# A fused retention and gated-MLP kernel: the first layer of batch 1 in seven half-size products, and the output product of batch 0 moved behind its gate

## The chip, the cores and the metric

The kernel runs on one core of a Trainium2 chip. The metric is the device time of one execution in microseconds. The kernel before took 510.05 us (median of three runs, 509.23 to 510.31). Five engines of the core work side by side, each on its own stream of instructions: TensorE (PE, with its weight loads shown apart as PEld), VectorE (DVE), ScalarE (ACT), GpSimd (POOL) and SyncE (SP, which here issues the DMAs).

## The reference, cut to what matters

```python
# q, k, v: (8 batches, 8 heads, 576 tokens, 64)
scores = q @ k.T / sqrt(64)
ret = scores * D                     # D[h, i, j] = gamma_h ** (i - j) for i >= j, else 0
x = (ret @ v) -> (8, 576, 512)       # heads side by side
h = relu(x @ w_in)                   # w_in (512, 1024)
u, v = h[..., :512], h[..., 512:]
v_n = (v - mean(v)) / sqrt(var(v) + 1e-6)
v_s = w_spatial @ v_n + b_spatial    # w_spatial (576, 576), over the tokens
out = (u * v_s) @ w_out              # w_out (512, 512)
```

All in float32. No softmax stands between the scores and their product with v, so the first half can be computed chunk by chunk with a carried state.

## The kernel before, in words

**One batch.** The 576 tokens are four chunks of 128 and a tail of 64. A chunk is loaded by DMA (tiles qk, kn, vv), its q and k are scaled, its scores are taken and masked (at), and the state of the heads (sh, st, decayed in dec) carries what earlier chunks leave. These are 64-row matmuls, in groups of 16 or 32, in the banks r. The result x goes to SBUF transposed. Then come the first layer (u and v), v normalised (vn, and vt1 for the tail), the spatial product with w_spatial (wsp, wtl) and the gate (u * v_s, called g below), and the output product, whose blocks are stored from the tiles o, vl, tail and u.

**Accuracy.** PE multiplies rounded numbers (type F32R). Each operand is kept as a rounded half and the rest, and each product is three matmuls: high by high, high by low, low by high (`mm3`, L571). So before a product takes an operand, ACT copies it into the rounded half and another engine subtracts that (type fp32r in the rows): a *split*.

**Two ways to a dense product.** The *plain* way takes a 512 x 512 product block by block: a tile of u is 12 matmuls of 288 columns, a tile of v for one chunk 12 of 512. The other takes it as *seven products of half size* instead of eight (`product_chain`, L860, parts A to E; `product`, L836): sums and differences of quarters of the weights, made once (`made_weight`, L336), by sums and differences of quarters of x or g, made in every batch (`plain_quarter`, L327, `summed_quarter`, L330). A product for one half of the rows is 6 matmuls, of 256 columns for v and 288 for u and the output; its results are added up by DVE in the tile u. Rows of such products read the tiles quarter, part, places and slot.

**Which batch goes which way.** `PLAIN = 2`: batches 0 and 1 have a plain first layer. Batch 0's output product is plain too (`f_chain`, L812); the output of batch 1 and all of batches 2 to 7 are seven products.

**The order.** It is written out by hand. `ORDER` (L44) holds batches 0 and 1 and the start of 2, `STEADY` is repeated for each later one, `LAST` ends it. Each word names a chain, and each time it stands there, `run` (L942) takes one step of that chain: one group of instructions. Every engine runs its instructions in that order, so the order of words sets every engine's queue; nothing is reordered later. The words used here (the table of makers is at L907): d, D, T, S load a chunk, a weight, a tail, w_spatial; w and s split weights; q, k, t, g, p, b are the steps of the retention; v is a chunk of v with its normalising; U, V, G, P are batch 0's u, spatial product, gate and split; y and X are u and the spatial product of a plain batch 1; F is a plain output product; W is a part of seven products (batch, kind, half, part); R and K make plain and summed quarters of x, Y and Z those of g; A makes weights of the seven products. Letters at the end (p, v, a) choose the engine: POOL, DVE, ACT. `BANKS` gives each product its PSUM bank m0 to m3.

**Rooms.** SBUF is full, so tiles share tags. The two big rooms slot0 and slot1 hold x and g of a batch in turns; `room` (L337) for making the weights of the output lies in slot0, the raw weights pass through `raw` and slot1.

All instructions are issued through one wrapper, so the trace gives line 204 for each (209 in the changed kernel); rows are told apart by tiles. In rows, m stands for the four banks, r for those of the retention, win and wout for the weights, slot for x or g of a batch, kn and qk for loaded chunks, qsct and tail for the tail.

Of the kernel before, what the change touches and what calls it, by code (L numbers as in the profile page):

```python
# [29 lines left out]
PLAIN = 2  # L30
WHOLE = 1
# [12 lines left out]
    d.0.0 z.40.1 c.a z.22.1 d.0.0 z.17.1 d.0.0 z.10.1 D.1.1 d.0.1 z.16.1 d.0.1 z.24.1 d.0.1 z.13.1 z.15.1 D.1.0  # L44
    z.39.1 g.0.0 D.1.2 g.0.0 q.0.0.p D.1.3 k.0.0.v d.0.2 p.0.0.va z.19.1 p.0.0.va z.26.1 D.0.1 z.23.1 w.1.1.vp
    p.0.0.va b.0.0 w.1.1.vp z.20.1 b.0.0 w.1.1.vp D.0.0 b.0.0 b.0.0 p.0.0.va d.0.3 w.1.1.vp k.0.1.p g.0.1 b.0.0
    D.0.2 w.1.1.vp z.2.1 p.0.0.va z.5.1 q.0.1.p b.0.0 p.0.1.aa w.1.1.vp z.33.1 p.0.1.aa w.1.0.vp z.27.1 g.0.1 z.25.1
    z.1.1 z.42.1 w.1.0.vp z.21.1 z.11.1 w.1.0.vp z.41.1 w.1.2.pp z.30.1 z.32.1 w.1.0.vp p.0.1.aa z.3.1 w.1.2.pp
    z.34.1 z.35.1 w.1.0.vp z.18.1 w.1.3.vp b.0.1 S z.4.1 b.0.1 w.1.3.vp w.1.0.vp T.0 z.8.1 p.0.1.aa b.0.1 S w.1.3.vp
    w.1.0.vp b.0.1 w.1.2.pp z.31.1 b.0.1 z.9.1 w.1.3.vp z.29.1 c.t z.37.1 k.0.2.a q.0.2.p z.38.1 w.1.2.pp g.0.2  # L50
    b.0.1 d.1.0 z.6.1 w.1.1.vp w.1.2.pp z.7.1 p.0.1.aa d.1.0 p.0.2.aa z.0.1 w.0.0.vp p.0.2.aa z.12.1 v.0.0 w.1.3.vp
    w.1.2.pp w.0.0.vp p.0.2.aa z.14.1 w.1.2.pp g.0.2 b.0.2 w.0.0.vp z.36.1 w.1.3.vp S v.0.1 w.0.1.vp p.0.2.aa
    w.1.3.vp w.0.0.vp v.0.0 k.0.3.a S w.0.1.vp v.0.0 m w.0.0.vp v.0.0 w.0.1.vp D.2.0 q.0.3.p b.0.2 v.0.0 d.1.0
    p.0.2.aa d.1.1 v.0.0 t.0.p t.0.p b.0.2 b.0.2 g.0.3 S w.0.2.pp p.0.3.ap w.0.1.vp s.1.p t.0.p z.28.1 w.0.2.pp
    p.0.3.ap v.0.1 b.0.2 g.0.3 p.0.3.ap v.0.1 b.0.2 q.1.0.p v.0.1 d.1.1 s.0.p p.0.3.ap s.1.p w.0.2.pp b.0.3 d.1.1
    g.1.0 w.0.1.vp b.0.3 v.0.1 b.0.3 k.1.0.p g.1.0 v.0.0 v.0.2 v.0.0 s.2.p v.0.2 s.0.p v.0.1 s.3.p b.0.3 w.0.0.vp
    w.0.2.pp s.2.p p.1.0.pp e.0.v T.1 v.0.0 v.0.2 e.0.v D.2.1 w.0.2.pp b.0.3 d.1.2 s.3.p v.0.2 v.0.1 D.0.3 b.0.3
    v.0.3 d.1.2 v.0.0 v.0.2 w.0.0.vp v.0.3 p.1.0.pp v.0.1 v.0.4 s.4.p v.0.2 v.0.4 p.1.0.pp w.0.2.pp v.0.4 k.1.1.p
# [12 lines left out]
    A.0.15.v v.1.3 G.1.1 A.0.8.v A.1.5.p e.1.v w.2.3.vp v.1.1 q.2.0.v P.0.1.p v.1.1 w.2.2.vv G.1.1 v.1.3 w.2.2.vv
    v.1.1 e.1.v v.1.3 k.2.1.a b.2.0 w.2.2.vv F.0.0.1 v.1.3 A.0.11.v v.1.1 F.0.0.1 P.1.1.v y.1.2.1 w.2.3.vp P.1.1.v
    w.2.2.vv A.0.4.v P.1.0.v F.0.0.0 p.2.0.vp y.1.2.1 p.2.0.vp v.1.1 p.2.0.vp b.2.0 v.1.1 y.1.3.0 w.2.3.vp F.0.0.0
    v.1.3 v.1.3 v.1.4 A.1.1.v y.1.3.0 v.1.4 v.1.3 A.1.0.v F.0.0.3 P.1.0.v A.1.2.p g.2.1 F.0.0.3 v.1.1 b.2.0 b.2.0
# [80 lines left out]
def retention_gmlp(ctx, tc, qkv, tails, w_in, w_sp, b_sp, w_out, terms, tmask, out):  # L155
# [87 lines left out]
    def load(b, c, steps=None):  # L243
# [32 lines left out]
    def normed(i):  # L276
        return keep(f"vn{i}", [P, NC, DH], F32R)
# [757 lines left out]
```

## Time and profile before

| | |
|---|---|
| median of three runs | 510.05 us (509.23 to 510.31) |
| the profiled execution | 510.43 us, of which the span of the trace is 508.7 us |
| mean granted clock of PE | 0.993 |
| PE busy | 498.9 us, 7335 matmuls |
| DVE, ACT, POOL busy | 397.1, 260.0, 152.6 us |
| batches 0 and 1, up to where the windows of a repeated batch begin | 0 to 211.4 us |
| one repeated batch, by the window of rows 2 | 59.3 us |

Each engine's busy time is what its instructions take on the trace; matmuls are pipelined and their ends are modelled, so the best measure of what a run of matmuls costs is the distance from the start of one group to the start of the next. Where a row ends in brackets, the engine stood idle ahead of it for that many microseconds, and the name behind the arrow is what ended the wait: an engine and a tile, a DMA, or "issue" where the profile shows nothing. In the 40 slices of the page PE is at 9 tenths or more in all but the first and the last, and the granted clock is full after the first slice.

### The profile page before, as it was taken

The page shows a single profiled execution, that of the slowest core. Times are in us where ns is not written, and L with a number is a line of the kernel's source. Part 1 is how long each engine was busy: PE and PEld are TensorE (multiplying, and loading weights), DVE is VectorE, ACT ScalarE, POOL GpSimd, SP SyncE. Part 2 cuts the span into 40 slices and gives each one's busy share as a digit, 9 for nine tenths or more (in the row PEclk, how much of TensorE's full clock was granted, in tenths as well). Part 3 has the DMA queues.
Part 4 walks back from the last instruction along what each step waited for, and adds up shares of the span by engine and source line. Part 5 has one row for each costly group of instructions (what it writes and reads, how often), then busy time and mean ns, then how long its engine had stood idle before and what let it go on. Part 6 is the DMA issues. An engine that isn't in the chain of part 4 may idle for free.

```text
span 508.7 us, 17035 instructions
## 1 busy us (share of the span) xinstructions
PE 498.9 (98%) x7335; PEld 472.7 (93%) x7335; DVE 397.1 (78%) x881; ACT 260.0 (51%) x587; POOL 152.6 (30%) x133
## 2 busy tenths in 40 slices
PE   7999999999899999999999999999999999999997
PEld 5778999999899999999999999999999999999996
DVE  3798898768699886788769785888767886788756
ACT  2798544745345562537326472455625574357513
POOL 1499634314027430245114250143302240020000
PEclk8999999999999999999999999999999999999999
DMA  8997522025415422162222441144220620011002
GB/s 299 405 296 248 157 80 73 1 79 138 160 41 151 172 78 84 40 189 85 64 85 78 152 143 54 37 146 150 83 86 27 195 93 3 1 39 56 2 1 93
DMA packets 29516, 55.52 MB, mean 109 GB/s; under 512 B 2945, under 2 KB 15361, under 8 KB 29186
## 3 DMA queue, kind: packets, MB, share of 16 engines
q1 hardware_dynamic: 29442, 54.45, 32.8%
q8 instruction: 57, 0.93, 0.8%
q14 instruction: 17, 0.14, 0.1%
HBM read 45.00 MB, written 9.44 MB: 107 GB/s over the span
## 4 chain that ended last, share of the span: by engine, by line
PE 89%; DVE 4%; DMA 2%; ACT 2%; issue 1%; SPq 0%; DVEq 0%; ACTq 0%
PE m L204 76%; PE r L204 13%; DVE u L204 2%; DMA kn<-in_qkv 1%; DMA fixed_terms<-in_terms 1%; DVE slot L204 1%; ACT slot L204 1%; DVE kn L204 1%; ACT dec L204 0%; ACT u L204 0%; ACT lent_wout L204 0%; SPq L204 0%; DVE x L204 0%; ACT f L204 0%; ACT win L204 0%
## 5 line engine op out<-in xcount | busy, mean ns | idle before, releaser
L204 PE MATMUL m<-wsp,vn 128*128 128x288 f32 x768 | 113.2, 296 | 0.5 <-issue 0.5
L204 PEld LDWEIGHTS m<-wsp,vn 128*128 128x128 f32 x768 | 105.1, 188 | 1.3 <-issue 0.7
L204 DVE TENSOR_TENSOR u<-m,u 128x288 f32<-128x288 f32 (+1 forms) x132 | 57.2, 439 | 19.3 <-PE m L204 12.3
L204 ACT COPY u<-m 128x288 f32<-128x288 f32 (+1 forms) x92 | 34.6, 385 | 38.3 <-PE m L204 30.1
L204 PE MATMUL m<-slot,win 128*128 128x288 f32 x336 | 50.5, 296 | 0.0
L204 PEld LDWEIGHTS m<-slot,win 128*128 128x128 f32 x336 | 46.5, 188 | 0.6
L204 POOL TENSOR_TENSOR slot<-u,slot 128x576 fp32r<-128x576 f32 x7 | 10.2, 1459 | 107.1 <-ACT slot L204 107.1
L204 DVE SCALAR_TENSOR_TENSOR u<-u,m 128x288 f32<-128x288 f32 x48 | 21.2, 451 | 24.8 <-PE m L204 24.6
L204 PE MATMUL m<-slot,wout 128*128 128x288 f32 x264 | 39.5, 295 | 0.4 <-issue 0.4
L204 PEld LDWEIGHTS m<-slot,wout 128*128 128x128 f32 x264 | 36.5, 188 | 0.8 <-issue 0.5
L204 PE MATMUL m<-win,slot 128*128 128x512 f32 (+1 forms) x168 | 35.3, 348 | 0.0
L204 ACT CAST slot<-u 128x576 fp32r<-128x576 f32 x32 | 21.4, 676 | 24.1 <-DVE u L204 23.8
L204 PEld LDWEIGHTS m<-win,slot 128*128 128x128 f32 x168 | 27.1, 188 | 4.2 <-DVE slot L204 0.2
L204 ACT CAST places<-u 128x576 fp32r<-128x576 f32 x21 | 14.2, 678 | 32.1 <-DVE u L204 31.8
L204 PE MATMUL m<-quarter,slot 128*128 128x256 f32 x216 | 29.7, 283 | 0.0
L204 ACT COPY r<-warm 1x2 f32<-1x2 f32 x32 | 4.9, 153 | 47.0 <-PE r L204 46.2
L204 PE MATMUL m<-wtl,vt 128*128 128x288 f32 (+1 forms) x128 | 27.5, 296 | 0.4 <-DVE vt L204 0.4
L204 DVE TENSOR_TENSOR at<-r,fixed_terms 128x512 f32<-128x512 f32 x32 | 21.8, 682 | 7.5 <-DMA fixed_terms<-in_terms 4.8
L204 POOL TENSOR_TENSOR kn<-kn,fixed_terms 128x512 f32<-128x512 f32 x15 | 15.7, 1048 | 39.2 <-DMA kn<-in_qkv 39.2
L204 PE MATMUL m<-slot,part 128*128 128x288 f32 x168 | 27.1, 300 | 0.4
L204 PEld LDWEIGHTS m<-quarter,slot 128*128 128x128 f32 x216 | 26.9, 188 | 0.4
L204 PE MATMUL m<-places,wout 128*128 128x288 f32 x168 | 26.7, 297 | 0.0
(166 smaller groups left out, 1213.1 us busy)
## 6 DMA issues: line engine op xcount, KB each, us to landing
qk<-in_qkv SPq DMA_DIRECT2D x30, 512.0 KB, 4.2
kn<-in_qkv SPq DMA_DIRECT2D x30, 256.0 KB, 5.0
vv<-in_qkv SPq DMA_DIRECT2D x30, 256.0 KB, 4.5
out<-u SPq DMA_DIRECT2D x28, 144.0 KB, 1.8
tail<-in_tails SPq DMA_DIRECT2D x8, 384.0 KB, 4.3
out<-o SPq DMA_DIRECT2D x18, 144.0 KB, 1.9
lent_slot<-in_w_in SPq DMA_DIRECT2D x4, 512.0 KB, 8.3
raw<-in_w_in SPq DMA_DIRECT2D x4, 512.0 KB, 10.9
```

Of the source, the lines that this page charges most:

```text
L204: ins = op(*args, **kw)
```

## The change

`PLAIN` becomes 1: batch 1's first layer is done as seven half-size products too. Its four quarters and sums of x are made in the two rooms by a table of their own, `places_of_first`. `SPARE = 2` keeps the double buffers of the retention for batches 0 and 1 as they were; `normed` gets a second pair of names for v from batch 1 on, in the same rooms. The rooms in which weights are made move: those of the first kind into the raw weights in slot1, the others into the rooms of vn0 and vn1. Batch 0's fourth output block leaves from the tile `tail` like every other batch's. `ORDER` is written anew throughout, `BANKS` too; `STEADY` and `LAST` differ in a few neighbouring words that change places.

```diff
-PLAIN = 2
-WHOLE = 1
+PLAIN = 1
+SPARE = 2
...
-    ... v.1.3 A.0.11.v v.1.1 F.0.0.1 P.1.1.v y.1.2.1 w.2.3.vp P.1.1.v
-    w.2.2.vv A.0.4.v P.1.0.v F.0.0.0 p.2.0.vp y.1.2.1 p.2.0.vp v.1.1 p.2.0.vp b.2.0 v.1.1 y.1.3.0 w.2.3.vp F.0.0.0
...
+    R.1.1.v F.0.0.3 R.1.2.v F.0.0.2 R.1.1.v F.0.1.3 A.2.7 A.2.9.v p.2.0.aa K.1.5.vv A.2.10 A.1.13.v F.0.1.1 F.0.1.3
+    K.1.7.vv A.2.12.v F.0.1.0 F.0.1.1 A.2.13.v K.1.7.vv R.1.2.v F.0.1.2 W.1.0.0.A R.1.3.v W.1.0.1.A K.1.5.vv R.1.3.v
...
-            vv = keep(f"vv{n % (3 if b < PLAIN else 2)}", [P, 512])
+            vv = keep(f"vv{n % (3 if b < SPARE else 2)}", [P, 512])
...
-    def normed(i):
-        return keep(f"vn{i}", [P, NC, DH], F32R)
+    def normed(i, b):
+        return keep(f"vn{i}{'b' if b else ''}", [P, NC, DH], F32R, tag=f"vn{i}")
...
+    places_of_first = {1: (1, 0, 0), 2: (1, 1, 0), 6: (1, 1, 1), 7: (1, 0, 1), 5: (0, 0, 0), 3: (0, 1, 1), 4: (0, 1, 0)}
...
-    def right(kind, n):
-        return place(*(places_of_g if kind == 2 else places_of_x)[n])
+    def right(b, kind, n):
+        return place(*(places_of_g if kind == 2 else places_of_first if b == PLAIN else places_of_x)[n])
...
     def made_weight(s, step, eng=po):
-        room = keep("room", [P, NCB, S], tag="slot0") if s == 2 else x32()
-        t = [room[:, k, :512].rearrange("p (a n) -> p a n", a=2) for k in range(4)]
+        if s == 0:
+            room = raw_v[:, 2 * S:2 * S + 4 * 512].bitcast(F32).rearrange("p (k n) -> p k n", k=4)
+        else:
+            room = keep(f"room{s}", [P, NC, DH], tag=f"vn{s - 1}")
+        t = [room[:, k].rearrange("p (a n) -> p a n", a=2) for k in range(4)]
...
-        if k == 3 and b < WHOLE:
-            return keep("early_out", [P, DH], tag="part")[:, :HALF]
...
-    for b in range(PLAIN, B - 2):
+    for b in range(SPARE, B - 2):
```

PE's queue in the middle of batch 0's output product, before. The first two rows are that product (g of batch 0 in slot0, by wout); then come the last matmuls of a tile of v of batch 1 (512 columns, x in slot1 by win) and a tile of its u.

```order
L204 MATMUL m1_87<-slot0_217,wout0_1100 128x288 x2
L204 MATMUL m1_87<-slot0_217,wout1_1118 128x288
L204 MATMUL m0_86<-win0_66,slot1_842 128x512
L204 MATMUL m0_86<-win1_67,slot1_842 128x512
L204 MATMUL m0_86<-win0_66,slot1_842 128x512
L204 MATMUL m2_88<-slot1_842,win0_66 128x288 x2
L204 MATMUL m2_88<-slot1_842,win1_67 128x288
```

PE's queue at the end of batch 0's output product, in the change:

```order
L209 MATMUL m0_86<-slot0_221,wout0_1143 128x288 x2
L209 MATMUL m0_86<-slot0_221,wout1_1184 128x288
L209 MATMUL m2_88<-win0_66,slot1_1496 128x256
L209 MATMUL m2_88<-win1_67,slot1_1496 128x256
L209 MATMUL m2_88<-win0_66,slot1_1496 128x256 x2
L209 MATMUL m2_88<-win1_67,slot1_1496 128x256
L209 MATMUL m2_88<-win0_66,slot1_1496 128x256
L209 MATMUL m1_87<-win0_66,slot1_1496 128x256
```

The output product of batch 0 is no longer interleaved with batch 1's first layer, which follows it in half products of six matmuls of 256 columns.

PE's queue at batch 0's spatial products (wsp by vn), before: the third piece, by the third chunk of v, and then a tile of v of batch 1 and the steps of a chunk of the retention, ahead of the fourth piece.

```order
L204 MATMUL m0_86<-wsp0_68,vn0_669 128x288
L204 MATMUL m0_86<-wsp1_69,vn0_669 128x288
L204 MATMUL m0_86<-wsp0_68,vn1_670 128x288
L204 MATMUL m1_87<-win0_66,slot1_842 128x512
L204 MATMUL m1_87<-win1_67,slot1_842 128x512
L204 MATMUL m1_87<-win0_66,slot1_842 128x512 x2
```

The same place in the change:

```order
L209 MATMUL m2_88<-wsp0_68,vn0_605 128x288
L209 MATMUL m2_88<-wsp1_69,vn0_605 128x288
L209 MATMUL m2_88<-wsp0_68,vn1_606 128x288
L209 MATMUL r1_91<-qk0_94 64x64 x16
L209 MATMUL r1_91<-vv0_110,kn0_95 64x64 x16
L209 MATMUL r0_90<-qsc1_228,st1_76 64x64
```

The tile of v of batch 1 is gone from between the pieces; the steps of the retention stay there.

DVE's queue at the normalising of batch 1's last chunk, before: the table for the output weights (room, from wout) stands between the steps of the statistics (sm) and the rounding of that chunk into vt1.

```order
L204 TENSOR_TENSOR room_1784<-wout0_1100,wout1_1118 128x512
L204 RECIPROCAL sm0_604<-sm0_604 64x1
L204 TENSOR_SCALAR sm0_604<-mv0_456,sm0_604 64x1
L204 TENSOR_SCALAR sm0_604<-sm0_604 64x1 x2
L204 TENSOR_TENSOR room_1784<-room_1784 128x512
L204 TENSOR_TENSOR dec0_78<-st0_75,fixed_terms_64 128x256
L204 TENSOR_TENSOR room_1784<-wout0_1100,wout1_1118 128x512
L204 TENSOR_TENSOR sh_77<-r1_91,dec0_78 128x256
L204 SCALAR_TENSOR_TENSOR vt1_72<-m1_87,sm0_604,vt1_72 64x512
```

The same steps in the change:

```order
L209 RECIPROCAL sm0_449<-sm0_449 64x1
L209 TENSOR_SCALAR sm0_449<-mv0_444,sm0_449 64x1
L209 TENSOR_SCALAR sm0_449<-sm0_449 64x1 x2
L209 TENSOR_TENSOR u_144<-m0_86,u_144 128x288
L209 TENSOR_TENSOR sh_77<-r1_91,dec0_78 128x256
L209 SCALAR_TENSOR_TENSOR vn1b_1791<-u_144,sm2_716,vn0b_1790 128x512
L209 SCALAR_TENSOR_TENSOR vt1_72<-m3_89,sm0_449,vt1_72 64x512
```

Where the table stood, there are additions of products into u and the rounding of another chunk. The last of the tables and the new quarters of x (x32, and their splits into slot1 and places0) stand further ahead on DVE, at the start of batch 1's first layer:

```order
L209 TENSOR_TENSOR room2_1367<-wout0_1143,wout1_1184 128x512
L209 TENSOR_TENSOR room2_1367<-room2_1367 128x512
L209 TENSOR_TENSOR slot1_1496<-x32_839,slot1_1496 128x2x288
L209 TENSOR_TENSOR places0_1563<-x32_839,places0_1563 128x2x288
L209 TENSOR_TENSOR x32_839<-x32_839 128x2x288
L209 TENSOR_TENSOR places0_1563<-x32_839,places0_1563 128x2x288
L209 TENSOR_TENSOR x32_839<-x32_839 128x2x288
L209 TENSOR_TENSOR slot1_1496<-x32_839,slot1_1496 128x2x288 x2
```

These differences and splits, of 576 elements for each partition, are on DVE's queue for batch 1 only in the change.

## Rows read from the trace of the kernel before

**Rows 1.** The page, busy time, share of the span and instructions of each engine.

```profile
PE 498.9 (98%) x7335; PEld 472.7 (93%) x7335; DVE 397.1 (78%) x881; ACT 260.0 (51%) x587; POOL 152.6 (30%) x133
```

**Rows 2.** Windows: stretch, busy us (instructions) of PE, PEld, DVE, ACT, POOL, clock, DMA, GB/s.

```profile
20.00:60.00 40.00, 39.76 (x795) 32.91 (x796) 36.73 (x83) 33.24 (x88) 34.54 (x32) 1.00 0.77 252
76.60:129.50 52.90, 52.51 (x708) 49.34 (x707) 39.09 (x81) 28.97 (x69) 17.09 (x12) 1.00 0.29 82
211.40:270.70 59.30, 59.17 (x917) 57.35 (x917) 46.83 (x108) 28.81 (x64) 17.39 (x15) 1.00 0.32 99
```

**Rows 3.** Timeline of PE at five waits, 120 to 170 us (start, length, operation, [idle]).

```profile
124.34 0.54 PE L204 MATMUL m<-wtl,vt 128*128 128x288 f32 x2 [0.40 <-DVE vt L204]
...
131.16 0.69 PE L204 MATMUL r<-qk 64*64 64x64 f32 x32 [0.88 <-DVE st L204]
...
135.01 0.67 PE L204 MATMUL m<-wsp,vn 128*128 128x288 f32 x3 [0.50 <-issue]
...
150.91 0.57 PE L204 MATMUL m<-slot,wout 128*128 128x288 f32 x3 [0.35 <-issue]
...
165.03 0.69 PE L204 MATMUL r<-vv,kn 64*64 64x64 f32 x32 [0.16 <-DVE kn L204]
```

**Rows 4.** Timeline of PE, 83 to 88 us, a full stream of plain products.

```profile
83.42 2.22 PE L204 MATMUL m<-win,slot 128*128 128x512 f32 x9
85.48 1.75 PE L204 MATMUL m<-slot,win 128*128 128x288 f32 x12
87.08 2.96 PE L204 MATMUL m<-win,slot 128*128 128x512 f32 x12
```

**Rows 5.** Timeline of PE, 169 to 171 us, half products of 256 columns.

```profile
169.07 1.56 PE L204 MATMUL m<-quarter,slot 128*128 128x256 f32 x12
170.47 0.62 PE L204 MATMUL m<-win,xt 128*128 128x512 f32 x2
```

**Rows 6.** Timeline of DVE ahead of two of these waits, 121 to 131 us.

```profile
121.39 1.78 DVE L204 TENSOR_TENSOR room<-wout,wout 128x512 f32<-128x512 f32 x1
...
129.44 0.43 DVE L204 TENSOR_TENSOR qsct<-tail,fixed_terms 128x256 f32<-128x256 f32 x1 [2.29 <-DMA tail<-in_tails]
...
130.08 0.69 DVE L204 TENSOR_TENSOR kn<-kn,fixed_terms 128x512 f32<-128x512 f32 x1 [0.21 <-DMA kn<-in_qkv]
```

**Rows 7.** Timeline of POOL and DVE, 160 to 165 us.

```profile
160.84 5.43 POOL L204 TENSOR_TENSOR slot<-x,slot 128x576 fp32r<-128x576 f32 x3 [1.56 <-ACT slot L204]
...
163.08 1.90 DVE L204 TENSOR_TENSOR kn<-kn,fixed_terms 128x512 f32<-128x512 f32 x1
```

**Rows 8.** Timeline of PE and DVE at batch 0's spatial products, 48 to 57 us.

```profile
48.72 1.86 PE L204 MATMUL m<-slot,win 128*128 128x288 f32 x12
...
56.52 0.66 PE L204 MATMUL m<-wsp,vn 128*128 128x288 f32 x3
...
54.65 0.75 DVE L204 SCALAR_TENSOR_TENSOR vn<-m,sm,vn 128x512 fp32r<-128x512 f32 x1
```

**Rows 9.** DVE without gaps: timeline, then groups by form (busy us, mean ns, idle).

```profile
147.71 0.75 DVE L204 TENSOR_TENSOR u<-u 128x576 f32<-128x576 f32 x1
148.38 0.75 DVE L204 TENSOR_TENSOR slot<-u,slot 128x576 fp32r<-128x576 f32 x1
...
124.32 1.29 DVE L204 TENSOR_TENSOR room<-room 128x512 f32<-128x512 f32 x2
...
164.90 0.74 DVE L204 TENSOR_TENSOR u<-m,u 128x256 f32<-128x256 f32 x2
...
L204 DVE TENSOR_SCALAR sm<-sm 128x1 f32<-128x1 f32 x64 | 13.7, 215 | 2.2
```

**Rows 10.** Timeline of PE, two groups of the retention one behind the other.

```profile
54.78 0.65 PE L204 MATMUL r<-qk 64*64 64x64 f32 x32
55.24 0.65 PE L204 MATMUL r<-vv,kn 64*64 64x64 f32 x32
```

**Rows 11.** The page, DMA issues: instructions, KB each, us from issue to landing.

```profile
tail<-in_tails SPq DMA_DIRECT2D x8, 384.0 KB, 4.3
```

More of the change, by code (lines that the diff above doesn't have):

```diff
@@ L49 @@
[L49 to L58, printed above, removed]
@@ L325, in split_quarter, with plain_quarter, summed_quarter @@
         yield
-    def plain_quarter(kind, n, eng=po):
-        yield from split_quarter(kind, n, of_sum(kind, *blocks[n]), eng)
-    def summed_quarter(kind, n, e1=ve, e2=ve):
+    def plain_quarter(b, kind, n, eng=po):
+        yield from split_quarter(b, kind, n, of_sum(kind, *blocks[n]), eng)
+    def summed_quarter(batch, kind, n, e1=ve, e2=ve):
         a, b, t = (of_sum(kind, *k) for k in sums[n])
@@ L384, in fetch @@
         else:
-            t = keep("raw", [P, NCB * S], I32)[:, i * 1024:(i + 1) * 1024] if i < 2 else keep(f"raw{i}", [P, 1024], I32)
+            if i >= 2:
+                t = keep(f"raw{i}", [P, 1024], I32)
+            elif kind:
+                t = raw_v[:, (1 - i) * 6 * S:][:, :1024]
+            else:
+                t = keep("raw", [P, NCB * S], I32)[:, i * 1024:(i + 1) * 1024]
             w = w_in if kind == 0 else w_out
@@ L730, in v_finish @@
         if sb < NC:
-            hi, lo = (normed(i)[:, sb] for i in range(2))
+            hi, lo = (normed(i, b)[:, sb] for i in range(2))
         else:
@@ L756, in vs_chain @@
         for sb in range(NC):
-            mm3(ps, [normed(i)[:, sb, ds] for i in range(2)], [wsp[i][:, sb, ts] for i in range(2)], sb == 0, False)
+            mm3(ps, [normed(i, 0)[:, sb, ds] for i in range(2)], [wsp[i][:, sb, ts] for i in range(2)], sb == 0, False)
             if db == 0 and t == 0:
@@ L834, in on, with product @@
         return {"p": po, "v": ve, "a": ac}[how]
-    def product(kind, n, m, ps, start, stop):
-        w, r = factor(kind, n), right(kind, n)
+    def product(b, kind, n, m, ps, start, stop):
+        w, r = factor(kind, n), right(b, kind, n)
         for k in range(2):
@@ L877, in product_chain @@
             for k, (p, to) in enumerate(((1, (0, 0)), (6, (0, 1)), (7, (1, 0)))):
-                product(kind, p, m, ps, k == 0, True)
+                product(b, kind, p, m, ps, k == 0, True)
                 yield
@@ L885, in product_chain @@
         elif part == "B":
-            product(kind, 5, m, ps, True, True)
+            product(b, kind, 5, m, ps, True, True)
             yield
@@ L889, in product_chain @@
             if not early:
-                product(kind, 3, m, ps, False, True)
+                product(b, kind, 3, m, ps, False, True)
                 yield
@@ L893, in product_chain @@
         elif part == "D":
-            product(kind, 3, m, ps, True, True)
+            product(b, kind, 3, m, ps, True, True)
             yield
@@ L898, in product_chain @@
         elif part == "C":
-            product(kind, 2, m, ps, True, True)
+            product(b, kind, 2, m, ps, True, True)
             yield
@@ L902, in product_chain @@
         else:
-            product(kind, 4, m, ps, True, True)
+            product(b, kind, 4, m, ps, True, True)
             yield
```

158 lines of the change are left out of this document (86 added, 72 removed).

## The prediction, made before the change was run

> **What bounds the kernel now.** I read the busy table first [rows 1]: PE has work for 498.9 of 508.7 us, DVE for 397.1. A busy PE is not yet a full one, so the table by stretches comes next [rows 2]. In the repeated batch (211.4 to 270.7) PE is busy for 59.17 of 59.30 us, DVE for 46.83: these batches are paced by PE, and the change leaves their matmuls alone. Whatever is won or lost ahead of them moves the end by as much. Ahead of them there are two kinds of place: 20 to 60 us, where DVE is 92% busy and PE still hardly waits, and 120 to 165 us, where PE loses time in five waits that no repeated batch has in that number [rows 3]. So the sum has two terms: the columns that PE no longer streams, and the waits that go, stay or come.
>
> **PE's work.** Batch 1 is the second batch with a plain first layer: 8 tiles of u with 12 matmuls of 288 columns, 4 tiles of v with 12 of 512, 96 and 48 matmuls. The change puts seven products in two halves there, 7 x 6 x 2 = 84 of 256 columns (v) and 84 of 288 (u). What one costs in a full stream is the distance from start to start: nine of 512 take 83.42 to 85.48, 0.229 us each, and twelve of 288 take 85.48 to 87.08, 0.133 each [rows 4]; twelve of 256 take 169.07 to 170.47, 0.117 each [rows 5]. Removed: 96 x 0.133 + 48 x 0.229 = 23.8 us. Added: 84 x 0.117 + 84 x 0.133 = 21.0 us. All of it is on PE, which sets the end: **-2.8 us**. The 64-row matmuls and every other product keep their number; the warm-up matmuls too.
>
> **Waits that go.** [rows 3] shows PE idle for 0.40, 0.88, 0.50, 0.35 and 0.16 us. Idle time counts from the modelled end of a matmul, and in a full stream a group ends 0.15 us behind the next start (1.75 long, the next 1.60 later, in [rows 4]); between starts the five cost 2.29 + 5 x 0.15 = 3.0 us. Behind them [rows 6]: at 121.39 DVE makes a table for the output weights, 1.78 us long, ahead of the rounding of the last chunk that PE waits for at 124.34; at 129.44 DVE stands for 2.29 us before the tail of batch 2 (a DMA), and the scores that PE needs at 131.16 come behind it. In the new order the tables of the output weights stand on DVE well ahead of batch 1's v, and the tail of batch 2 is scaled on POOL. The wait at 150.91 is not of this kind: PE waits for the sums and differences of g, which the change leaves where they are. It stays, at 0.5 us, and is set against the -3.0. The one at 165.03 hangs on a DVE scaling of k that lies beside three roundings on POOL [rows 7]; DVE does these roundings now and POOL one difference ahead of them, and I leave 0.2 of it. **-3.0, of which +0.7 stays.**
>
> **Waits that may come.** First, 50 us. PE now reaches the spatial products of batch 0 sooner, because the twelve products of 512 columns that lay between the third and the fourth piece (0.229 x 12 = 2.7 us) are gone from there. From the first u tile at 48.72 to the fourth piece at 56.52 were 7.8 us; now 5.1, so 53.8 [rows 8]. DVE's roundings for it ended at 54.65 + 0.75 = 55.40. DVE's order is new too: two operations of 512 columns fewer stand ahead of that rounding, 1.3 us, so it ends near 54.1. Between no wait and 1.6 us, if DVE's new order gains nothing; I take 0.5.
>
> Second, the new preparation of batch 1's x. From batch 2's first scores to the product that needs the third sum, DVE has 34 operations: 12 of 576 columns, 15 of 512, 3 of 288, 4 of 256. Back to back those of 576, 512 and 256 cost 0.67, 0.65 and 0.37 us [rows 9], those of 288 by these about 0.4: 8.0 + 9.8 + 1.2 + 1.5 = 20.5 us. PE has 120 matmuls of 288, 24 of 256 and seven groups of sixteen 64-row products at 0.46 [rows 10], 16.0 + 2.8 + 3.2 = 22.0 us. So DVE arrives 1.5 us early if it never waits, and on the way it waits for PE (three tiles of u) and for ACT (seven roundings). Nothing if all is hidden; 4 x 1.2 - 1.5 = 3.3 us if four of its operations run against POOL at 1.2 us more each (below). I take 0.5, nearer to the count.
>
> Third, batch 1's normalised v. Counted in the same way, from the same scores to the last chunk that the first spatial product takes, DVE has 14 of 576, 24 of 512, five statistics of that width, 7 of 288, 17 of 256 and 25 of one or two columns at 0.215 [rows 9]: 9.4 + 15.6 + 3.2 + 2.8 + 6.3 + 5.4 = 42.7 us. PE has 195 matmuls of 288, 84 of 256, 8 of 512 and fifteen groups, 25.9 + 9.8 + 1.8 + 6.9 = 44.4 us. A slack of 1.7 us over 44, with DVE at 96%. That DVE can run near this without PE waiting is what 20 to 60 us shows at 92% [rows 2]; in the same place before, 76.6 to 129.5, it had 39.09 us in 52.9. ACT's part (scales, roundings) waits for POOL's last table there too, since the tables now live in the room of v. Between 0 and 3 us; I take 0.5.
>
> **Edits at nothing.** Batch 0's output products are the same 96 matmuls in another place. Their eight stores move with them on SP, and batch 2's tail load [rows 11] now stands behind two of them, since the fourth output block leaves from the tile into which the tail is loaded. It lands 4.3 us after its issue, and PE has 13 us of products before its first use; without that cover PE would lose the 2.3 us of [rows 6] again. Warm-up, weight order and the new room for the tables at the start shift work between DVE, POOL and ACT (ACT has 53 instructions more, POOL 13, DVE 3 in all). ACT hides that at 51% of the span; 1 us either way. The swaps in the repeated batches: 0, at most 0.3.
>
> **Sum.** -2.8 - 3.0 + 0.7 + 0.5 + 0.5 + 0.5 = -3.6 us. The profiled execution took 510.43 us, 508.7 of it the span; it lies 0.4 above the median of the runs, 510.05. So 506.8 against its own time, **506.4** against the median.
>
> **POOL and DVE.** [rows 7] shows what speaks against this change: while POOL rounds three tiles from 160.84 on, DVE's scaling of k takes 1.90 us, otherwise 0.69 [rows 6]. The Trainium skill, "SBUF — State Buffer", section "Who interferes with whom", says that a DVE instruction with two SBUF inputs and a GpSimd instruction that reads SBUF lock each other out for the whole instruction; the trace agrees with it in that stretch. By that rule the new differences and roundings of x, all with two SBUF inputs, would pay each time that POOL works beside them.
>
> **The rivals.** *All is hidden.* DVE is quicker than I count and only the wait for g stays: -2.8 - 3.0 + 0.7 = -5.1, so 505.0, with a better start 504. For it: DVE's spacing in [rows 9] is already that of full streams. Against it: 96% of an engine over 44 us. *The saving is eaten.* The columns go, but the new waits at the three places come to 3 to 4 us instead of 1.5: 510.05 - 5.1 + 3 to 4, that is 508 to 509, and over 509 where the start slips by its 1 us too. For it: the third place, where the chain runs over DVE, ACT and POOL by turns. Against it: DVE then has to lose 3 us more than counted. *Slower: DVE becomes the bound against POOL.* The place is the preparation and normalising of batch 1, 44 us long, with 17 POOL operations where as much of PE's work had 12 beside it. DVE has 1.7 us to spare; each collision costs 1.90 - 0.69 = 1.2 us. From seven collisions on, 8.4 - 1.7 = 6.7 us of wait eat more than the 5.1 us to be won, and nine or ten give 510.05 - 5.1 + 10 = 515; with seven and the start at its bound 512. For it: [rows 7]. Against it: POOL has nothing to do in the new order from the last u tile to batch 2's second scores, where most of the new differences lie.
>
> **How the numbers follow.** The forecast, 505.2 to 507.8, gets 0.48; all hidden, 503.6 to 505.2, 0.23; eaten, 507.8 to 511, 0.20; slower, above 511, 0.09. The range leaves out the slow case and a little at either end: 503.6 to 510.2. A measurement of this kernel tells about 0.2%, 1 us, from no change. Faster by more than that is below 509.0: the first two and a third of the third, 0.48 + 0.23 + 0.07 = 0.78. Within it, to 511.1: 0.13. Slower: 0.09.
>
> **What would show it.** In the new profile the first layer of batch 1 should stand in groups of 256 and 288 columns at 0.117 and 0.133 us from start to start, with no group of 512 but those of the tail. The waits for the rounding of the tail chunk and for batch 2's fourth scores should be gone. DVE should show over 90% from the end of batch 0's gating to batch 1's first spatial product. The repeated batches should keep 59.3 us [rows 2]. I am wrong if PE has waits of over a microsecond for DVE's differences of x or for normalised v, if DVE's differences there take 1.2 us and more, or if the first 50 us have moved.

## The result, and the profile after

The changed kernel takes 514.18 us (median of 8 runs, 512.6 to 517.75); the kernel before took 510.34 on the same chip (8 runs, 509.23 to 513.75). The ratio is 1.0084 (95% interval 1.006 to 1.0108): it is slower by 3.8 us, where 3.6 us less were forecast.

To compare traces I use the profiled execution of after and a second one of the kernel before, because both ran at the full clock throughout; in the first execution of before, which the rows ahead of the prediction come from, the granted clock was at half from 8.4 to 15.2 us. Spans and mean granted clocks, first of before (second execution), then of after:

```profile
core 0: 507.4 us, clock 1.000
```

```profile
core 0: 510.8 us, clock 1.000
```

The busy row of the page of after answers to [rows 1]. PE has 0.3 us less work in 2.1 us more of span; DVE, ACT and POOL have 8, 15 and 18 us more:

```profile
PE 498.6 (98%) x7359; PEld 472.3 (92%) x7359; DVE 404.7 (79%) x884; ACT 274.8 (54%) x640; POOL 170.5 (33%) x146
```

The windows of after answer to [rows 2] (columns as there). The two in the middle are the preparation of batch 1's x and its normalised v; the last is a repeated batch:

```profile
20.00:60.00 40.00, 36.48 (x732) 29.93 (x733) 33.60 (x74) 29.14 (x71) 34.65 (x30) 1.00 0.81 277
84.50:107.80 23.30, 21.98 (x285) 20.61 (x283) 22.47 (x34) 15.66 (x39) 5.87 (x4) 1.00 0.28 82
107.80:129.30 21.50, 21.09 (x388) 19.64 (x389) 20.16 (x57) 18.16 (x49) 13.13 (x12) 1.00 0.42 127
213.80:273.10 59.30, 59.20 (x917) 57.38 (x917) 46.59 (x108) 28.65 (x63) 17.10 (x16) 1.00 0.32 99
```

The repeated batch keeps its 59.30 us. From 20 to 60 us PE is now busy for 36.48 instead of 39.76 us, and in the preparation DVE has work for 22.47 of 23.30 us. So the loss lies ahead of batch 2, in the start and in batch 1.

PE's waits by what ended them, in all, count and longest, of after:

```profile
PE r L209 <- issue: 3.1, 2, 2.7
PE m L209 <- DVE u L209: 2.4, 4, 1.3
...
```

The waits for `vt` and `st` of [rows 3] are gone. In their place stand two waits of 3.1 us that no engine ended, and four on DVE's `u`, the longest 1.3 us. PE's rows at the two largest, and the columns of the new first layer:

```profile
27.79 0.28 PE L209 MATMUL r<-lent_wout 64*64 64x64 f32 x3
30.79 0.68 PE L209 MATMUL r<-lent_wout 64*64 64x64 f32 x29 [2.72 <-issue]
...
37.08 0.62 PE L209 MATMUL r<-at,lent_wout 64*64 64x64 f32 x27 [0.36 <-issue]
...
89.15 9.75 PE L209 MATMUL m<-slot,wout 128*128 128x288 f32 x72
98.74 2.22 PE L209 MATMUL m<-win,slot 128*128 128x256 f32 x18
...
108.21 0.98 PE L209 MATMUL m<-quarter,places 128*128 128x256 f32 x6 [1.33 <-DVE u L209]
```

From 89.15 to 98.74, 72 of the 96 matmuls of batch 0's output product now run in one piece, 9.59 / 72 = 0.133 us each as in [rows 4], and groups of 256 columns follow them. At 27.79 a group of 32 stops after three matmuls and goes on 3 us later.

**Where the time went.** I add up the usual distance from start to start of all matmuls ahead of a place (the median of the trace: 0.117 us at 256 columns, 0.132 at 288, 0.232 at 512; 0.0137 on average for a 64-row one) and take it from the time at which the place starts. What is left is PE's lag: waits, and whatever a matmul costs beyond its usual distance. Beside it stand the long waits (over 0.25 us beyond the usual distance) in the stretch that ends there, and how often PE goes from 64-row groups to wide matmuls in that stretch ("switches"):

| place | lag before | lag after | long waits before, after | switches before, after |
|---|---|---|---|---|
| batch 0's first tile of u | 12.98 | 15.19 | 4.3, 6.1 | 13, 15 |
| batch 0's seventh tile of u, behind its spatial products | 15.03 | 18.78 | 0, 0.9 | 4, 5 |
| batch 1's first spatial product | 16.58 | 24.76 | 0, 2.0 | 3, 7 |
| batch 2's first layer begins | 19.88 | 27.29 | 1.9, 0.7 | 2, 4 |
| last matmul | 37.51 | 44.22 | 2.1, 1.45 | 26, 26 |

The start loses 3.75 us and batch 1's first layer 4.4; the stretch behind it, where the waits that were to go stood, gives 0.8 back. In all the lag grows by 6.71 us. The columns give 2.9 back (sum of usual distances 466.0 before, 463.1 after), so the last matmul starts 3.8 us later; the spans differ by 3.4. The long waits explain 2.9 of the 6.7; nine more switches and small losses remain. What a switch costs is the first question for the chip.

### The profile page after: what moved, and what is told of

The parts are those of the page before. It is cut to its first block, busy times and chain, and to the rows that moved or that the text cites. A ratio compares the mean times of both kernels' runs of the same rounds, so it can differ in the third digit from the quotient of the medians.

```text
span 510.8 us, 17173 instructions
## 1 busy us (share of the span) xinstructions
PE 498.6 (98%) x7359; PEld 472.3 (92%) x7359; DVE 404.7 (79%) x884; ACT 274.8 (54%) x640; POOL 170.5 (33%) x146
## 4 chain that ended last, share of the span: by engine, by line
PE 84%; DVE 8%; DMA 3%; issue 2%; POOL 1%; ACT 1%; SPq 1%; DVEq 0%; ACTq 0%; POOLq 0%
PE m L209 72%; PE r L209 12%; DVE u L209 3%; DVE slot L209 2%; DMA kn<-in_qkv 1%; DMA vv<-in_qkv 1%; DVE places L209 1%; DVE x L209 1%; SPq L209 1%; DVE quarter L209 1%; ACT slot L209 1%; POOL lent_slot L209 1%; DVE at L209 0%; DVE lent_slot L209 0%; ACT places L209 0%
## 5 line engine op out<-in xcount | busy, mean ns | idle before, releaser
L209 PE MATMUL m<-wsp,vn0b 128*128 128x288 f32 x448 | 91.2, 296 | 0.0
L209 PEld LDWEIGHTS m<-wsp,vn0b 128*128 128x128 f32 x448 | 71.6, 188 | 0.4
L209 PE MATMUL m<-wsp,vn1b 128*128 128x288 f32 x224 | 65.9, 294 | 0.0
L209 ACT COPY u<-m 128x288 f32<-128x288 f32 (+1 forms) x104 | 39.1, 384 | 40.0 <-PE m L209 32.7
L209 PE MATMUL m<-slot,win 128*128 128x288 f32 x276 | 42.5, 297 | 0.0
L209 PEld LDWEIGHTS m<-wsp,vn1b 128*128 128x128 f32 x224 | 42.1, 188 | 0.0
L209 PEld LDWEIGHTS m<-slot,win 128*128 128x128 f32 x276 | 38.3, 188 | 0.5
L209 POOL TENSOR_TENSOR qk<-qk,fixed_terms 128x512 f32<-128x512 f32 (+1 forms) x18 | 23.5, 1308 | 34.2 <-PE r L209 33.7
L209 POOL TENSOR_TENSOR places<-x,places 128x576 fp32r<-128x576 f32 x6 | 10.3, 1717 | 65.2 <-ACT places L209 65.2
L209 POOL TENSOR_TENSOR x<-x 128x576 f32<-128x576 f32 x12 | 19.4, 1615 | 25.0 <-DVE places L209 24.6
```

Source lines behind the costliest of these rows:

```text
L209: ins = op(*args, **kw)
```

## The experiments

All kernels but three are the changed kernel with words of its order moved or given to another engine, three of them with warm-up matmuls added; "before again", "one switch fewer in the kernel before" and "two waits taken from the kernel before" start from that one. A ratio is against the kernel before on the same chip, with its 95% interval.

**Four more switches in every repeated batch.** Groups of six wide matmuls are put between the 64-row groups that stood together:

```diff
-W.a.0.0.A b.b.0 ... p.b.1.vp W.a.0.0.B W.a.0.0.A
+W.a.0.0.A W.a.0.0.B b.b.0 ... p.b.1.vp W.a.0.0.A
...
```

> The changed kernel, with four more switches between 64-row and wide matmuls in each of the four repeated batches: one wide product is put into each of four groups of the retention, nothing else moves. Theory C: 4 x 0.23 = 0.92 us for each batch, 59.3 to 60.2 us, 3.7 us in all. Rival (switches are free): 59.3 us for a batch and the same time.

520.89 us (520.74 to 522.93), 1.0225 [1.0206, 1.0244]. Between the first layers of batches 3, 4, 5 and 6 lie 60.92, 60.89 and 60.91 us; in after 59.31, 59.31 and 59.33. Four switches cost 1.60 us: **0.40 each**, more than I had expected of it. PE's rows at one of the places, in after and then in this kernel:

```profile
226.55 0.67 PE L209 MATMUL r<-vv,kn 64*64 64x64 f32 x28
227.15 1.67 PE L209 MATMUL m<-quarter,slot 128*128 128x256 f32 x12
228.66 0.87 PE L209 MATMUL m<-win,slot 128*128 128x256 f32 x6
```

```profile
228.75 0.64 PE L208 MATMUL r<-qk 64*64 64x64 f32 x30
229.31 0.97 PE L208 MATMUL m<-quarter,slot 128*128 128x256 f32 x6
230.21 0.27 PE L208 MATMUL r<-qk,sh 64*64 64x64 f32 x2
...
230.92 0.67 PE L208 MATMUL r<-vv,kn 64*64 64x64 f32 x28
231.52 0.98 PE L208 MATMUL m<-quarter,slot 128*128 128x256 f32 x6
232.34 0.52 PE L208 MATMUL m<-win,slot 128*128 128x256 f32 x3
```

No row has an idle time, and yet six matmuls that take 6 x 0.117 = 0.70 us in a stream take 0.90 from 229.31 to 230.21; the rest falls on the groups beside them. A view of waits can't show this cost. The Trainium skill, "TensorEngine Tiling (Array Packing)", section "Key Properties", says that a change of the tiling mode drains TensorE; the trace agrees, with 0.40 us for each way there and back.

**Six switches fewer** in the first two batches (57 become 51), by putting steps of the retention side by side:

```diff
-U.1 ... w.2.0.pv b.1.0 v.0.4
+b.1.0 U.1 ... w.2.0.pv v.0.4
-b.1.1 s.5.p V.0.0 b.1.1
+s.5.p V.0.0 b.1.1 b.1.1
...
```

> The changed kernel, with the 64-row groups of the retention brought together in six places between 45 and 126 us: PE goes 51 times from 64-row matmuls to wide ones instead of 57 (the kernel before: 48). Theory C (a switch costs): in both traces a change from wide to 64-row matmuls and back shows 0.09 + 0.14 us beside the usual distances from start to start, so six fewer give 6 x 0.23 = 1.4 us. Rival: the 0.23 us are a filling of the pipeline that shows up elsewhere when groups stand together, or the retention's steps then wait for ACT and DVE in between: 0 to 1 us slower.

514.82 us (514.43 to 515.09), 1.0098 [1.0084, 1.0113]: no gain. From batch 0's first u to its output product the lag grows by 3.38 us instead of 4.59, 1.2 for three switches; long waits are 0.25 of it (1.17 instead of 1.42), so a switch taken away gives 0.3 to 0.4. In the preparation it grows by 5.74 instead of 4.89: there the same words put PE ahead of DVE, as PE's rows of this kernel show.

```profile
105.11 2.50 PE L207 MATMUL m<-quarter,slot 128*128 128x256 f32 x16 [0.47 <-DVE slot L207]
108.97 0.97 PE L207 MATMUL m<-quarter,places 128*128 128x256 f32 x6 [1.36 <-DVE u L207]
```

The rest is the start, where this execution lost 1.5 us more than after (below).

**POOL's three splits given to DVE.** DVE and then POOL in after, ahead of the wait at 108.21 (the answer to [rows 7]):

```profile
101.12 0.75 DVE L209 TENSOR_TENSOR places<-x,places 128x576 fp32r<-128x576 f32 x1
102.46 3.62 DVE L209 TENSOR_TENSOR slot<-x,slot 128x576 fp32r<-128x576 f32 x2
106.00 1.82 DVE L209 TENSOR_TENSOR places<-x,places 128x576 fp32r<-128x576 f32 x1
...
101.93 1.75 POOL L209 TENSOR_TENSOR qk<-qk,fixed_terms 128x512 f32<-128x512 f32 x1 [17.80 <-PE r L209]
103.64 1.82 POOL L209 TENSOR_TENSOR quarter<-room,quarter 128x512 fp32r<-128x512 f32 x1
105.42 1.79 POOL L209 TENSOR_TENSOR wout<-room,wout 128x512 fp32r<-128x512 f32 x1
107.17 1.80 POOL L209 TENSOR_TENSOR part<-room,part 128x512 fp32r<-128x512 f32 x1
```

DVE's split of x takes 0.75 us alone and 1.81 (3.62 for two, and 1.82) while POOL works; POOL's operation on `qk` takes 1.75 us here and 1.30 at 118.40. The edit moves the splits of `quarter`, `wout` and `part`:

```diff
-A.1.8.p ... A.2.11.p ... A.2.8.p
+A.1.8.v ... A.2.11.v ... A.2.8.v
```

> The changed kernel, but three roundings of made weights (steps 8 and 11 and 8 of the second and third kind) go from POOL to DVE, where they stand behind the last split of batch 1's x. Theory A (collisions): in the changed kernel three splits of x take 1.82 to 1.86 us on DVE, from 102.46 to 107.8, because POOL rounds at the same time; without POOL beside them they take 0.75 each, the third ends 3.2 us sooner, PE's wait of 1.33 us for the first sum of batch 1's v falls under 0.2, and the whole is 1.5 to 2 us shorter. Theory B (DVE is simply full there): DVE now has 3 x 0.6 = 1.8 us more of its own, so the wait only moves into batch 1's normalised v, and the time stays within 0.5 us of the changed kernel.

514.2 us (513.36 to 517.46), 1.0094 [1.0067, 1.012]: no gain. DVE and then PE of this kernel:

```profile
105.48 2.51 DVE L207 TENSOR_TENSOR slot<-x,slot 128x576 fp32r<-128x576 f32 x2
107.91 0.75 DVE L207 TENSOR_TENSOR places<-x,places 128x576 fp32r<-128x576 f32 x1
```

```profile
109.40 0.87 PE L207 MATMUL m<-quarter,places 128*128 128x256 f32 x6
...
114.67 0.74 PE L207 MATMUL m<-win,xt 128*128 128x512 f32 x2 [0.25 <-DVE u L207]
116.73 0.98 PE L207 MATMUL m<-quarter,places 128*128 128x256 f32 x6 [0.63 <-DVE u L207]
```

The wait of 1.33 is gone: from the end of batch 0's output product to batch 1's first product for u the lag grows by 1.23 instead of 3.13, so the collisions cost 1.9 us. But behind it new waits on DVE's `u` appear, and up to the first spatial product 4.33 instead of 4.89 are left, 0.56 won. DVE has no room there (it is busy for 28.54 of the 29.99 us from 101.77 on): a wait that is taken away in front comes back behind.

**All of it together.** First, the two edits above, one step of the weights' tables later on DVE and another from POOL to DVE:

```diff
-b.1.1 d.1.3 A.0.5.v p.1.1.pa ... v.0.4 V.0.0 ... A.2.5.p G.1.3 ... A.2.6.v
+b.1.1 d.1.3 p.1.1.pa ... v.0.4 A.0.5.v V.0.0 ... G.1.3 ... A.2.5.v A.2.6.v
```

> The first two edits together, and two more: a difference of weights on DVE (1.76 us long at 55.4 us) behind the rounding of batch 0's tail chunk, and one table step from POOL to DVE at 82 us so that DVE's split of g is not beside it. If collisions and switches are both real and add up: 1.75 + 1.4 and 0.3 + 0.5 for the two, some 4 us under the changed kernel, that is about the kernel before. If DVE is simply full, 1.4 us under it or nothing.

514.04 us (513.13 to 515.25), 1.0085 [1.0068, 1.0101]. Second, the three splits on DVE, the later step, eleven switches fewer (46), some by joining groups in `STEADY` and `LAST`, and the warm-up told of below:

```diff
+z.43.11 t.0.p
...
-b.2.3 W.1.1.1.E ... Z.1.5.vv g.3.0 W.1.2.0.A
+W.1.1.1.E W.1.1.1.B b.2.3 g.3.0 b.2.3 ... Z.1.5.vv W.1.2.0.A
...
-b.b.3 b.b.3 d.c.1 ... X.a.1.0 p.c.0.vp X.a.1.1
+b.b.3 b.b.3 p.c.0.vp d.c.1 ... X.a.1.0 X.a.1.1
...
```

> The changed kernel with the warm-up matmuls of the run beside it, the three roundings on DVE, one DVE difference of weights behind the rounding of batch 0's tail, and 46 switches instead of 57 (three fewer between 45 and 90 us, three fewer between batches 2 and 3, one fewer in each repeated batch, one in the last). If all add up: 1.3 for the clock, 0.5 for the roundings, 11 x 0.40 = 4.4 for the switches, 6 us under the changed kernel, 508 us. If DVE sets the pace wherever an order gets tighter: 2 to 3 us under it.

514.04 us (513.53 to 515.33), 1.0081 [1.0063, 1.0099]. Neither gained, against my sums. Both hold edits that single runs show to trade one wait for another (the first the switches saved in the preparation, the second the groups joined in `STEADY` and the warm-up). Their traces show where the gain went. In the first the lag grows by 0.9 us less than in after between batch 0's first u and batch 1's first spatial product, but it is 2.2 larger at that u, behind a standstill and a half clock (below). In the second the lag at the last matmul is 0.9 below that of after, but the warm-up itself takes 2.55, and from batch 2's first layer on long waits grow from 1.45 to 6.3 us, while five fewer switches save 2.0 there. Most of them are waits for ACT's copy into `o`:

```profile
PE m L205 <- ACT o L205: 3.8, 5, 0.8
```

If the long waits and 0.40 us for each switch are taken from the lag that grows behind batch 2's first layer, 4.5 to 5.6 us are left in each of the 14 traces, with 21 to 42 switches there and 1.45 to 6.7 us of waits.

**The standstill at 28 us.** Eleven warm-up matmuls of 512 columns are put ahead of it:

```diff
-t.0.p
+z.43.11 t.0.p
```

> The changed kernel with eleven warm-up matmuls of 512 columns more, ahead of the tail scores of batch 0 at 26 us. In five traces of the changed order PE stands still for 2.5 to 3.4 us at 28 us, always at the same matmul, and in four of the five the granted clock is at half (1.2 GHz) for 3.4 to 6.8 us from 31 to 32 us on. Theory D: the half clock comes of that standstill and costs 1.3 us and more in most runs; with work in its place PE reaches the matmul when its instructions are there, the standstill is under 0.5 us, the clock stays full, and the median falls by 1.3 us, to near the 512.6 to 513.2 us of the runs with a full clock. Rival: the clock falls anyway, or the eleven matmuls (2.6 us) only push everything back: no change or 1 to 2 us slower.

514.14 us (513.2 to 515.73), 1.0082 [1.006, 1.0105]. PE's rows:

```profile
27.47 2.77 PE L207 MATMUL m<-wsp 128*128 128x512 f32 x11 [0.66 <-DVE f L207]
31.62 0.65 PE L207 MATMUL r<-lent_wout 64*64 64x64 f32 x32
```

The group of 32 runs through, so the standstill is gone; but the warm-up takes 11 x 0.232 = 2.55 us and the lag at batch 0's first u falls by 2.49 (15.19 to 12.70). Nothing is won. Four of the six runs have a mean granted clock of 1.000, two of 0.993. A cheaper fill was to decide whether the start is also held by something else:

```diff
-t.0.p
+z.43.44 t.0.p
...
-pe.matmul(ps, idle[:, :P], idle, start=True, stop=True)
+w = P if n > 1 else 512
+pe.matmul(ps[:, :w], idle[:, :P], idle[:, :w], start=True, stop=True)
```

> The run with eleven warm-up matmuls of 512 columns, but as 44 of 128 columns: the same columns, 33 matmuls (66 instructions with their weight loads) more. Theory E (PE ran out of instructions): the places where PE stood still without a cause in the profile lie 256 instructions apart and end 1.1 to 1.7 us behind a 16 KB load of instructions, so with 66 instructions more ahead of it PE reaches the end of what is loaded sooner, and the standstill that the eleven had removed comes back, 0.8 to 2 us long, at about matmul 475, inside or just behind the 44. Rival (the standstill of the changed kernel was a wait for data, which the eleven matmuls filled): no standstill over 0.5 us between 26 and 32 us.

516.08 us (515.61 to 516.49), 1.0117 [1.0094, 1.014]. The 44 matmuls of 128 columns took 4.9 us from start to start, 0.112 each, about what 256 columns take. So this fill was twice as long as meant. No standstill shows beside it, but that doesn't decide the question.

```profile
27.69 5.13 PE L207 MATMUL m<-wsp 128*128 128x128 f32 x44 [0.70 <-DVE f L207]
32.75 0.46 PE L207 MATMUL r<-tail 64*64 64x64 f32 x16
```

What the standstill is: PE's 14,718 records come with 58 transfers of the instruction queue in the page of after, 0.95 MB, which is 254 records and 16 KB for each.

```profile
q8 instruction: 58, 0.95, 0.8%
```

Waits without a releaser in the middle of a group come at matmul 475, 602 and 981 in after, at 2127 and 2382 in before: distances of 127, 379, 1146 and 255, multiples of some 127 matmuls with their weight loads. At 28.32 one such transfer begins, 0.94 us long, 0.25 us after PE's last modelled end; PE goes on 1.5 us after the transfer's. The other traces bear this out: the ten stops at 602, 2127 and 2382 or one beside them come in kernels of five different orders, and all end 1.2 to 1.7 us behind such a transfer; matmul 475 starts 1.3 us or more behind this one in every trace, and 1.3 to 1.6 in the seven with the standstill. With the fills PE comes to it only at 31.50 us (11 matmuls) and 33.58 us (44), 2.4 and 4.1 us behind the transfer, and doesn't stop. So I take it that PE has run out of instructions. The Trainium skill, "Runtime: NRT & Kernel Launch", section "Instruction fetch mechanics", gives blocks of 16 KiB, 256 instructions, fetched ahead and mostly hidden; the size agrees, and the hiding fails here for 2.7 us. Whether other transfers stand in its way was tried by moving three loads of w_spatial behind the first load of batch 1's second chunk and one of w_out behind the next:

```diff
-g.0.2 S ... w.1.2.vv S ... w.0.0.pp S ... w.0.0.pp D.2.0 ... d.1.1 ... d.1.1
+g.0.2 ... w.1.2.vv ... w.0.0.pp ... w.0.0.pp ... d.1.1 S S S ... d.1.1 D.2.0
```

> The changed kernel with four loads (three of four parts of w_spatial and one of w_out, 1.4 MB) issued behind the first load of batch 1's second chunk, at 27 us or later instead of 20 to 26 us; all engines keep their order but for SP. Theory E: the 16 KB of instructions that PE lacks at 27.9 us were asked for some 4 us sooner and stood behind these loads; with less ahead of them their load starts before 27 us instead of at 28.3, and the standstill of 2.9 us shrinks under 1.5 us. Rival (PE waits there for data or an engine): it stays at 2.5 to 3.4 us. What the time does is another matter, since the splits of w_spatial come later: within 2 us of the changed kernel either way.

515.32 us (514.39 to 517.36), 1.0116 [1.0093, 1.014]. The standstill stays:

```profile
31.75 0.69 PE L207 MATMUL r<-lent_wout 64*64 64x64 f32 x29 [2.59 <-issue]
```

The DMA engines were as full as before until 34 us, so the edit did not empty them. It doesn't support the theory, and it can't exclude it. Why the block comes late is open.

All seven profiles with after's start and no fill have this wait, 2.3 to 3.2 us long. In six of them PE's granted clock then goes to half, 1.2 GHz, for 3.4 to 6.8 us. Windows of the kernel with the splits on DVE, and then of after, which was the one without:

```profile
31.00:37.60 6.60, 5.89 (x40) 4.40 (x39) 3.86 (x10) 1.98 (x7) 4.81 (x5) 0.50 0.68 241
```

```profile
31.00:37.60 6.60, 6.24 (x160) 4.78 (x155) 5.82 (x14) 4.13 (x10) 5.84 (x7) 1.00 0.80 268
```

At batch 0's first u the first of these lags 3.4 us more than after, and the five others with a half clock 1.4 to 2.2 more. That fits the eight runs of after: the profiled one, 512.6 at a clock of 1.000, is the fastest, and the times rise as the mean clock falls, to 517.75 at 0.990.

**One switch fewer in each repeated batch of the kernel before**, by joining a group of the next batch's first chunk to the one ahead (its load and its scaling move ahead with it):

```diff
-b.b.3 d.c.1 ... X.a.1.0 p.c.0.vp X.a.1.1
+b.b.3 p.c.0.vp d.c.1 ... X.a.1.0 X.a.1.1
```

> The kernel before, with one switch fewer in each of the four repeated batches: the state update of the next batch's first chunk, which stands alone between wide products, joins the group of 64-row matmuls ahead of it. In the run with four more switches a batch took 60.9 us instead of 59.3, 0.40 us for each, more than the 0.23 expected. Theory C with 0.40: 4 x 0.40 = 1.6 us less, a batch of 58.8 us. Rival (the extra time of that run were waits that its order brought, and a switch alone costs 0.23 or nothing): 0 to 0.9 us less.

513.11 us (510.8 to 514.49), 1.0055 [1.0034, 1.0076]: slower. PE's rows:

```profile
271.96 2.23 PE L201 MATMUL m<-slot,part 128*128 128x288 f32 x12 [0.76 <-ACT o L201]
...
377.05 0.40 PE L201 MATMUL m<-wsp,vn 128*128 128x288 f32 x1
378.46 1.62 PE L201 MATMUL m<-wsp,vn 128*128 128x288 f32 x11 [1.01 <-issue]
```

The group that was moved had been PE's work while ACT copied into `o`, behind its cast of a sum of g; without it PE waits 0.76 us there, 3.0 in the four batches, and such a batch takes 59.68 us instead of 59.23. And at 377 us, behind the longer 64-row run, PE stops in the middle of a group as at 28 us. Here a saved switch didn't pay, because its place was needed as cover.

**The two waits taken from the kernel before**, without any of its columns: the tail of batch 2 loaded earlier and scaled on POOL, a step of the output weights' table and a scaling of k later on DVE.

```diff
-A.2.5.v b.2.1 ... v.1.4 X.1.0.2 T.2 ... t.2.v y.1.0.0 X.1.0.3 k.2.3.v
+T.2 ... b.2.1 ... v.1.4 A.2.5.v X.1.0.2 ... t.2.p y.1.0.0 X.1.0.3 ... k.2.3.v
```

> The kernel before, with only the waits taken away that the change was to remove: a difference of output weights on DVE goes behind the rounding of batch 1's tail chunk, batch 2's tail is loaded earlier and scaled on POOL, one scaling of k goes behind the state's sum. The prediction counted 2.3 us for these waits beside the one at 150 us. If they were real and nothing takes their place: 1.0 to 1.6 us less (0.55 at 123 us and 0.45 to 1.09 at 130 us in two traces; the one at 134 us is no wait of this kind by theory E and stays or moves). If the next wait takes their place: no change.

508.83 us (507.58 to 509.64, 12 runs), 0.9977 [0.9962, 0.9991]: the fastest kernel of this study, faster than both. PE's waits in the second execution of before, then here:

```profile
...
PE r L204 <- DMA tail<-in_tails: 0.7, 1, 0.7
PE m L204 <- issue: 0.6, 1, 0.6
PE m L204 <- DVE vt L204: 0.4, 1, 0.4
PE r L204 <- DVE st L204: 0.2, 1, 0.2
...
```

```profile
...
PE r L202 <- DVE kn L202: 1.4, 1, 1.4
PE m L202 <- issue: 0.5, 1, 0.5
PE r L202 <- issue: 0.4, 1, 0.4
...
```

The waits for `vt` and `st` are gone. (The one for a tail is batch 0's at 28.74, which the edit doesn't touch.) From the last part of batch 0's output product to batch 1's first one the lag grows by 1.08 instead of 2.36, 1.3 less.

**Before again**, for a trace at the full clock:

> The kernel before once more, for its granted clock. In its first profile the clock was at half from 8.4 to 15.2 us. If that is usual for it, a second trace shows it too and a span near 508.7; if it was chance, the clock is full and the span is shorter by 1 to 3 us, and the changed kernel's profile (full clock throughout) has hidden that much of the loss.

509.22 us, the execution used above; its clock is full and its span 1.2 us shorter than the first one's. In it the wait at 135.01 of [rows 3] is absent, and the one at 150.91 comes at 149.13 and costs 0.90 us beyond the usual distance. The waits of this trace at the place where after stands still:

```profile
27.33 0.74 PE L204 MATMUL m<-win,slot 128*128 128x512 f32 x2 [0.23 <-POOL win L204]
28.74 0.46 PE L204 MATMUL r<-tail 64*64 64x64 f32 x16 [0.68 <-DMA tail<-in_tails]
```

**The changed kernel mended**: the three splits on DVE, three switches fewer from 45 to 90 us, and one step of a weights' table behind batch 0's rounding of v.

```diff
-U.1 ... b.1.0 v.0.4 ... A.0.5.v p.1.1.pa ... A.1.8.p ... A.2.11.p ... A.2.8.p
+b.1.0 U.1 ... v.0.4 ... p.1.1.pa ... A.0.5.v ... A.1.8.v ... A.2.11.v ... A.2.8.v
...
```

> The changed kernel with the three roundings on DVE, one DVE difference behind the rounding of batch 0's tail and three switches fewer between 45 and 90 us; nothing else of the earlier runs. By the traces of those: 0.6 at the preparation of x, 3 x 0.40 for the switches and 0.3 for the tail, 2 us under the changed kernel, near 512 us, still above the kernel before. If the gains eat each other as in the run that combined everything: under 1 us.

512.26 us (511.87 to 514.68), 1.0055 [1.0035, 1.0074]: 1.9 below after, though the intervals of the two ratios overlap. From batch 0's first u to its output product its lag grows by 2.58 instead of 4.59 us, of which long waits are 0.37 instead of 1.42, and from there to the first spatial product by 4.33 instead of 4.89: 2.6 us. It stays behind the kernel before.

## Why the prediction was wrong

**The columns: right.** -2.8 was forecast, -2.9 measured.

**A term was missing: the switches.** "The 64-row matmuls and every other product keep their number" is true and left out their neighbours. PE goes from 64-row groups to wide matmuls 57 times instead of 48, and the sum put this at nothing without counting it; 9 x 0.40 = 3.6 us by the price of four more in a batch, 2.9 by that of three fewer with the waits set apart (0.32): as much as the columns save or more. This is the largest single error. It could be counted in PE's queue before the run; its price could not be read from a view of waits, since in a group PE counts as busy, but 0.23 us of it stands in the distances between starts.

**"Edits at nothing" failed at the start.** I took 0.5 us for the place at 50 us and put the new start at nothing, 1 us either way. By batch 0's seventh tile of u after has lost 3.75 us: three switches (1.2) and 2.7 of long waits, among them a standstill of 2.9 and one of 0.6 against 0.8 and 0.4 of waits that before has at 27 to 29 us. The place at 50 us itself was sized about right (the lag grows by 0.80 instead of 0.49 across the third and fourth piece). I had looked at how DVE and POOL share the start and not at whether PE's instructions are there.

**The preparation of x: the term was mis-sized.** I took +0.5 of a range that reached 3.3; the collisions cost 1.9. I argued that POOL has nothing to do up to batch 2's second scores, where most of the new differences lie. That holds (POOL is idle for 17.80 us up to 101.93), but three splits of x come behind these scores, and there POOL has four operations from 101.93 to 108.97, three of them weight splits. The count of 1.5 us to spare was right in that DVE is busy for 22.47 of 23.30 us, which is why moving the splits to DVE won 0.56 and not 1.9.

**Normalised v: right in the waits.** Behind 108.21 there is no long wait up to the first spatial product; the lag still grows there, by 1.88, and four of the seven switches of that row of the table lie there, 1.6 us.

**The waits that go: right in kind, too large.** The two at 124.34 and 131.16 are gone in after, and taken away alone they are worth 1.2 us, where I had counted 1.6 for them. Those at 135.01 and 150.91 I gave to DVE's queue and to the sums of g; both are marked "issue" and end 1.5 and 1.3 us behind a transfer of PE's instructions, and the first is absent in the second execution of the same kernel. So I take them for standstills.

**The sum.** Between forecast and measurement lie 3.6 + 3.8 = 7.4 us by the medians: 2.9 to 3.6 for switches, 3.7 because long waits grew by 2.9 where I had them fall by 0.8, less 0.1 for the columns; 0.2 to 0.9 are left in small pieces. The signs that I named for being wrong came: a wait of over a microsecond (1.33 at 108.21), splits of 1.82 us, and a start that moved. So did most of those for being right: the groups at their distances, DVE over 90% busy, the waits for the tail chunk and the fourth scores gone. They say nothing of the switches. Of the rivals, "slower: DVE becomes the bound against POOL" has the right sign and place for 1.9 of this; its time, 512 to 515, came out by luck, mostly from terms that it did not name.

**What stays open:** why PE's instructions come late at 28 us, whether the start would be faster without that, and whether nine switches less in the changed kernel, with no new wait, would win back what they cost: no run takes nine away without bringing waits.

## What to carry to other kernels

Count in PE's queue how often it goes between 64-row groups and full-width matmuls, and give that a price: a change that saves columns can lose more by scattering small groups. Before a term is put low because an engine has nothing to do in a stretch, list that engine's rows up to the end of the work that it could disturb. Where two engines have no room left, a removed wait comes back behind; taking the few waits out of the kernel as it stood won 0.23% that the larger change did not.

## What the runs showed of the hardware

- Going from 64-row matmuls to 128-row ones and back costs 0.40 us in all where four more were put into a batch, and gives 0.3 to 0.4 where three were taken away, without any idle time in the rows.
- PE stands 2.3 to 3.2 us in the middle of a group around a 16 KB transfer of its instruction queue, and goes on 1.3 to 1.6 us behind the transfer's end; in six of seven profiles a granted clock of one half follows for 3.4 to 6.8 us.
- A matmul of 128 columns takes 0.112 us in a stream, one of 256 columns 0.117.
- A two-input operation from SBUF takes 1.82 us on DVE beside POOL and 0.75 alone, and one of POOL's on 512 columns 1.75 beside DVE and 1.30 elsewhere.
